# Layer 0's three later norms as small steps at fixed projection units, two engines' order written out over 17 units, and a bias load moved into attention

## The chip, the cores and the metric

The kernel runs on one core of a Trainium2 chip. The metric is the device time of one execution in microseconds, and the figure quoted is the median of the runs. Before the change it is 3485.43 us over three runs (3485.06 to 3486.84). The engines are called by the names of the profile: PE multiplies matrices, DVE does elementwise work and reductions, ACT evaluates functions and copies, POOL does small elementwise work, and SP and ACT also issue transfers.

## The reference

Two layers, each a pre-norm attention block and a pre-norm two-matrix block, over 2048 tokens of width 512. The same weights serve both layers:

```python
x = A_x                                    # (1, 2048, 512)
for _ in range(2):
    x = x + attention(layernorm(x), wqkv, wo)          # 32 heads of 16
    x = x + mish(layernorm(x) @ w1 + b1) @ w2          # inner width 1792
```

The layer norm subtracts the row's mean and divides by the root of its variance plus 1e-5. The bias `b1` is used only in the second block.

## The kernel before, in words

Every large product is made of three matmuls. An operand is split into a high part (a copy rounded to the matmul's type, on ACT) and a low part (the difference, on DVE), and high times high, high times low and low times high are summed (`mm3`, lines 159 to 164; `mm3_by_kind`, lines 152 to 157, does all four of the first kind, then all four of the second, then the third). `split_psum` (lines 148 to 150) makes both parts from a PSUM bank: one ACT copy, then one DVE subtraction.

The 2048 tokens are four chunks `c` of 512 (four row tiles of 128 each). Layer 0 begins with the projections. Each entry `(m, c)` of a list `order` is one unit: product `m` (0 to 3 are q, 4 to 7 are k, each 128 columns wide) of chunk `c`, 12 matmuls of 128x512 into one of three PSUM banks (tag "s"), a `split_psum` into a tile `pt`, and a transfer of `pt` to memory (`scr`). An entry `("v", c)` is four such blocks of 12 matmuls whose results go to `vst`. In layer 0 the list is: units 0 to 5 for chunk 0 (products 0, 4, 1, 5, 2, 6), units 6 to 9 for chunk 1 (0, 4, 1, 5), unit 10 (3, 0), units 11 and 12 for chunk 2 (0, 4), unit 13 (7, 0), units 14 and 15 for chunk 1 (2, 6), units 16 and 17 for chunk 3 (0, 4), then four more q and k units, the v blocks, and the rest.

A unit needs its chunk's normalised rows, transposed and split, as `th` and `tl`. So chunk 1's norm must be complete by unit 6, chunk 2's by unit 11, chunk 3's by unit 16. Chunk 0's norm is `first_norm` (from line 656, called at line 728), written out by hand. The norms of chunks 1 to 3 go through `norm_parts` (lines 166 to 202): first the statistics of all four row tiles (`bn_stats` and `bn_aggr`, lines 177 and 178), one small addition and one POOL power (lines 173 and 174), then for each row tile the subtraction and scaling `xn` (line 196), four PE transposes of 128x128 (line 201), and a `split_psum` into `th` and `tl`. `steps` hangs the parts on units: a part is written ahead of the unit with that number.

The raw weights are loaded by SP in pieces of 256 columns (`make`, line 115) into three buffers with the tag "raw", which the `pt` tiles share, and split on ACT (line 121) and DVE (line 126). The pieces 0 and 2 serve products 0, 1, 4 and 5; the pieces 1 and 3 serve products 2, 3, 6 and 7; the pieces 4 and 5 are v.

What each engine does next is decided by a planner when the program is built: it goes through a simulated time and gives each engine, among the instructions that it takes as ready, the one that stands first in the program. The chip then runs each engine's list in that order. An `Order` object ties each instruction passed to it behind the one passed before on the same engine, so that the planner cannot exchange them. `front` is such an object. Before the change it holds the first loads, all of `first_norm`, the split of the weight pieces 0 and 2, the matmuls of units 0 and 1, and the statistics (lines 177 and 178) of chunks 1 to 3. Everything else in the projections is left to the planner.

After 18 units the matmuls of the row maxima begin between the projections (`some_max`; lines 272, 290 and 305): they need `ks` and `qs`, which SP loads back from `scr`. Attention of layer 0 (`att.run`) follows: 512 steps, with an order written out for PE, DVE and ACT, and `hooks[s]` called at step `s`. The second block (`mlp`) then uses the bias tile `b1t` (line 598).

Of the kernel before, what the change touches and what calls it, by code (L numbers as in the profile page):

```python
# [18 lines left out]
P = 128  # L19
# [30 lines left out]
def kernel(ctx: ExitStack, tc: tile.TileContext, x, wqkv, wo, w1, b1, w2, out):  # L50
# [94 lines left out]
        nc.sync.dma_start(t.bitcast(F32), wparts[kind, j])  # L145
        return t

    def split_psum(hi, lo, src):
        nc.scalar.activation(hi, src, AF.Copy)
        nc.vector.tensor_tensor(lo, src, hi.bitcast(F32), op=ALU.subtract)  # L150

    def mm3_by_kind(acc, pairs, pe=lambda ins: ins):
        n = len(pairs)
# [12 lines left out]
    def norm_parts(src, nm, got, key, tag, fine=False, o=lambda ins: ins):  # L166
        st = tmp.tile([P, NCH, 6], F32, tag="st", name=f"st{nm}")
        mv = tmp.tile([P, NCH, 2], F32, tag="mv", name=f"mv{nm}")
        ve = tmp.tile([P, NCH], F32, tag="ve", name=f"ve{nm}")
        rs = tmp.tile([P, NCH], F32, tag="rs", name=f"rs{nm}")  # L170

        def rstd(t, n):
            nc.vector.tensor_scalar(ve[:, t : t + n], mv[:, t : t + n, 1], EPS, None, op0=ALU.add)
            nc.gpsimd.tensor_tensor(rs[:, t : t + n], ve[:, t : t + n], mhalf[:, t : t + n], op=ALU.pow)

        def stats(t):
            o(nc.vector.bn_stats(st[:, t], src[:, t]))
            o(nc.vector.bn_aggr(mv[:, t], st[:, t]))

        if not fine:  # L180
            for t in range(NCH):
                stats(t)
            rstd(0, NCH)
            yield
        th = b8([P, KT, CW], F32R, f"th{nm}")
        tl = b8([P, KT, CW], F32R, f"tl{nm}")
        got[key] = (th, tl)
        if fine:
            stats(0)
            rstd(0, 1)  # L190
        for t in range(NCH):
            if fine and t + 1 < NCH:
                stats(t + 1)
                rstd(t + 1, 1)
            xn = t512("f", f"xn{nm}{t}")
            nc.vector.tensor_scalar(
                xn, src[:, t], mv[:, t, 0:1], rs[:, t : t + 1], op0=ALU.subtract, op1=ALU.mult
            )
            tp = pbank(tag, f"tp{nm}{t}")
            for k in range(KT):  # L200
                nc.tensor.transpose(tp[:, ts(k, P)], xn[:, ts(k, P)], ident)
            split_psum(th[:, :, ts(t, P)], tl[:, :, ts(t, P)], tp.rearrange("p (k n) -> p k n", k=KT))
            yield
# [230 lines left out]
    def qkv(l, wts, tt, order, before, first=None, vst=None):  # L434
        scr = [dram.tile([2, P, S], F32R, name=f"scr{l}{m}") for m in range(2 * NCH)]
        vscr = dram.tile([NG, P, NKT, HG * VW], F32, name=f"vscr{l}")
        att = Attention(l, scr, vscr)
        if vst is None:
            vst = padded(l)
        chained = False  # L440
        done, left = 0, sum(NCH if m == "v" else 1 for m, _ in order)

        def some_max():
            nonlocal chained
            if done == 2 * NCH and left < AHEAD and att.nm < AHEAD:
                chained = True
                att.tick()
                att.max_pair()
                att.max_one()
                att.max_one()  # L450

        for i, (m, c) in enumerate(order):
            for fn in before.get(i, ()):
                fn()
            th, tl = tt[c]
            chained = chained or (l == 1 and i >= 11)
            pe = att.order if chained else lambda ins: ins
            if m == "v":
                for t in range(NCH):
                    acc = pbank("s", f"va{l}{c}{t}")  # L460
                    mm3(
                        acc,
                        [
                            (th[:, k, ts(t, P)], tl[:, k, ts(t, P)], wts[4 + k // 2][:, 0, k % 2], wts[4 + k // 2][:, 1, k % 2])
                            for k in range(KT)
                        ],
                        pe=pe,
                    )
                    left -= 1
                    st = vst[:, t % 2]  # L470
                    nc.scalar.activation(st[:, :, 0:DH], acc.rearrange("p (h d) -> p h d", d=DH), AF.Copy)
                    nc.sync.dma_start(
                        vscr[:, :, c * NCH + t, :].rearrange("g p n -> p g n"),
                        st.rearrange("p (g h) w -> p g (h w)", g=NG),
                    )
                    some_max()
            else:
                w = wts[m // 2]
                pt = tmp.tile([P, 2, CW], F32R, tag="raw", name=f"pt{l}{m}{c}", bufs=3)
                acc = pbank("s", f"qk{l}{c}{m}")  # L480
                (mm3_by_kind if l == 0 and i < 2 else mm3)(
                    acc,
                    [(w[:, 0, k, ts(m % 2, P)], w[:, 1, k, ts(m % 2, P)], th[:, k], tl[:, k]) for k in range(KT)],
                    pe=first if first and i < 2 else pe,
                )
                left -= 1
                split_psum(pt[:, 0], pt[:, 1], acc)
                nc.scalar.dma_start(
                    scr[m][:, :, ts(c, CW)].bitcast(F32).rearrange("a p n -> p a n"), pt.bitcast(F32)
                )  # L490
                if m in (0, 4):
                    done += 1
                    if done >= 2 * NCH - 2 and done % 2 == 0:
                        edge = (NCH - 1) * CW
                        for _ in att.prep_qk(0, *((edge, S) if done == 2 * NCH else (0, edge))):
                            pass
                some_max()
        att.prep_v(0)
        return att
# [152 lines left out]
    def steps(before, at, parts):  # L652
        for i in at:
            before.setdefault(i, []).append(lambda: next(parts, None))
# [69 lines left out]
    load_qkv(0, wts, (0, 2), later=splits, stores=stores, lo="dve", o=front)  # L724
    for c in range(1, NCH):
        xc.append(load_x(c, front))
    front(nc.sync.dma_start(b1t, b1.rearrange("(f p) -> p f", p=P)))
    first_norm(xc[0], tt, splits, front)
    wait = []
    load_qkv(0, wts, (1, 3), later=wait, stores=stores, lo="dve")  # L730
# [7 lines left out]
        at(i, lambda j=j: load_qkv(0, wts, (j,), later=wait, stores=stores, lo="dve"))  # L738
    for n in range(6):
        at(19 + n, lambda n=n: stores[n]())  # L740
    for c, at in ((1, range(1, 7)), (2, range(6, 12)), (3, range(11, 17))):
        steps(before, at, norm_parts(xc[c], f"q0{c}", tt, c, "n", o=front))
    for l in range(2):
        if l == 0:
            order = [(m, 0) for m in (0, 4, 1, 5, 2, 6)] + [(m, 1) for m in (0, 4, 1, 5)] + [(3, 0)]
# [25 lines left out]
        def divide(c):  # L771
            next(work[c], None)
# [18 lines left out]
        for c, load, inv, div in ((0, 30, 22, 20), (1, 28, 21, 15), (2, 10, 7, 5)):  # L791
            hooks[STEPS - load] = lambda c=c: behind(c, att.order)
            hooks[STEPS - inv] = lambda c=c: invert(c)
            for k in range(KT):
                hooks[STEPS - div + k] = lambda c=c: divide(c)
        att.run(hooks)
        o = att.order
        behind(3, o)
# [67 lines left out]
```

## Time and profile before

| | before |
|---|---|
| median of three runs | 3485.43 us |
| the profiled execution's own time | 3488.07 us |
| its span, first to last instruction | 3486.3 us |
| mean granted PE clock over the span | 0.997 |
| end of the first norm, start of the first projection matmul | 12.14 us |
| last projection matmul of layer 0, start of attention | about 178.3 us |

The page gives for each engine the busy time, then the span in 40 slices, the transfer queues, and the chain of work that ended last, followed back from the last instruction. A row of a timeline has the start, the duration, the engine, the line of the kernel, the operation, its output and inputs, their shapes, and a count (x4) where like instructions are merged; in square brackets stand the idle time of the engine before it and what ended it. PE's matmuls overlap, so the distance between two starts tells more than a duration. "PEclk" is the share of PE's full clock that was granted. "SPq" and "ACTq" rows are transfers being issued.

### The profile page before, as it was taken

What the parts mean: (1) busy time and instruction counts of PE and PEld (TensorE: products, weight loads), DVE (VectorE), ACT (ScalarE), POOL (GpSimd) and SP (SyncE); (2) the same over time, 40 slices, a digit from 0 to 9 for tenths busy, and PEclk for the clock granted to TensorE, in tenths of its full rate; (3) what the DMA queues carried; (4) which work ended last, traced back from release to release, by engine and by line L of the source; (5) the groups of instructions that cost most, each with busy time, mean ns of one, the idle gap of its engine ahead of it and who ended that gap; (6) DMA issues with size and microseconds to landing.
All of it is one profiled execution on the core that took longest, in us unless ns stands there. A gap on an engine that the chain in (4) does not pass through costs nothing.

```text
span 3486.3 us, 71314 instructions
## 1 busy us (share of the span) xinstructions
PE 3453.0 (99%) x29075; PEld 1916.8 (55%) x29075; DVE 3002.5 (86%) x4155; ACT 2554.8 (73%) x4781; POOL 444.2 (13%) x441
## 2 busy tenths in 40 slices
PE   9999999999999999999999999999999999999999
PEld 6644444444444444887776444444444444458887
DVE  5699999999999996666637999999999999966565
ACT  3189889889889987344421898988988998973444
POOL 1000000000000001344410000000000000013544
PEclk9999999999999999999999999999999999999999
DMA  7641312223122115400254202112020221154000
GB/s 248 230 97 44 81 42 74 51 63 80 45 57 51 34 55 133 168 13 13 85 191 162 52 15 46 25 36 38 23 55 15 45 35 27 55 149 152 13 13 25
DMA packets 131864, 247.40 MB, mean 71 GB/s; under 512 B 30928, under 2 KB 72400, under 8 KB 116432
## 3 DMA queue, kind: packets, MB, share of 16 engines
q1 hardware_dynamic: 110960, 186.21, 21.2%
q10 hardware_dynamic: 20576, 56.63, 4.2%
q8 instruction: 229, 3.75, 0.5%
q14 instruction: 99, 0.81, 0.1%
HBM read 149.43 MB, written 92.27 MB: 69 GB/s over the span
## 4 chain that ended last, share of the span: by engine, by line
DVE 71%; PE 19%; POOL 3%; DMA 2%; ACT 2%; issue 2%; SPq 0%; DVEq 0%; POOLq 0%; ACTq 0%
DVE mxv L305 32%; DVE mxv L290 32%; POOL hb L607 2%; DVE al L608 1%; PE qk L162 1%; PE h L163 1%; PE h L164 1%; PE mo L164 1%; PE h L162 1%; PE qk L163 1%; PE qk L164 1%; PE mo L162 1%; PE mo L163 1%; POOL hb L604 1%; PE va L162 1%
## 5 line engine op out<-in xcount | busy, mean ns | idle before, releaser
L354 ACT ACTIVATE p<-sp 128x512 f32<-128x512 f32 x4096 | 2134.9, 598 | 242.0 <-PE pn L272 138.9
L305 DVE TENSOR_REDUCE mxv<-pn 128x1 f32<-128x512 f32 x2048 | 1306.5, 677 | 13.0 <-PE pn L272 12.2
L290 DVE TENSOR_REDUCE mxv<-pm 128x2 f32<-128x1024 f32 x1024 | 1242.0, 1213 | 68.4 <-PE pm L272 68.2
L352 PE MATMUL sp<-qs,ks 50*128 50x512 f32 x4096 | 1293.2, 448 | 1.8 <-ACT p L354 1.6
L378 PE MATMUL pv<-p,va 128*32 128x256 f32 x16384 | 1200.1, 389 | 0.0
L352 PEld LDWEIGHTS sp<-qs,ks 50*128 50x128 f32 x4096 | 571.3, 184 | 714.5 <-ACT p L354 629.6
L272 PE MATMUL pn<-ks,qs 48*128 48x512 f32 x2048 | 826.0, 450 | 1.5 <-DVE mxv L305 1.5
L378 PEld LDWEIGHTS pv<-p,va 128*32 128x32 f32 x16384 | 378.4, 108 | 548.1 <-issue 432.6
L272 PE MATMUL pm<-ks,qs 48*128 48x512 f32 x2048 | 438.7, 423 | 2.0 <-DMA ks<-scr 1.2
L272 PEld LDWEIGHTS pn<-ks,qs 48*128 48x128 f32 x2048 | 365.7, 184 | 8.7 <-DVE mxv L305 3.0
L317 POOL CAST nh<-nm 128x16 fp32r<-128x16 f32 x64 | 12.7, 198 | 2394.4 <-DVE nm L312 2394.4
L272 PEld LDWEIGHTS pm<-ks,qs 48*128 48x128 f32 x2048 | 194.0, 185 | 66.5 <-issue 8.1
L162 PE MATMUL mo<-w,ah 128*128 128x512 f32 x448 | 176.9, 396 | 4.1 <-DVE ah L606 3.1
L604 POOL TENSOR_TENSOR hb<-hb,he 128x512 f32<-128x512 f32 x112 | 153.6, 1371 | 198.3 <-DVE he L601 195.0
L163 PE MATMUL mo<-w,ah 128*128 128x512 f32 x448 | 175.3, 391 | 0.0
L607 POOL TENSOR_TENSOR hb<-hb,hr 128x512 f32<-128x512 f32 x112 | 158.4, 1415 | 131.7 <-DVE ah L606 126.9
L163 PE MATMUL h<-tlm,w 128*128 128x512 f32 x448 | 174.7, 390 | 0.0
L164 PE MATMUL h<-thm,w 128*128 128x512 f32 x448 | 174.7, 390 | 0.0
L162 PE MATMUL h<-thm,w 128*128 128x512 f32 x448 | 174.6, 390 | 0.0
L600 ACT ACTIVATE he<-he 128x512 f32<-128x512 f32 x112 | 70.8, 632 | 137.3 <-DVE he L599 136.2
L602 ACT ACTIVATE hr<-he 128x512 f32<-128x512 f32 x112 | 70.9, 633 | 134.7 <-DVE he L601 74.5
L608 DVE TENSOR_TENSOR al<-hb,ah 128x512 fp32r<-128x512 f32 x112 | 103.8, 927 | 75.1 <-POOL hb L607 73.7
(130 smaller groups left out, 2601.2 us busy)
## 6 DMA issues: line engine op xcount, KB each, us to landing
scr<-pt ACTq DMA_DIRECT2D x64, 512.0 KB
ks<-scr SPq DMA_DIRECT2D x168, 128.0 KB
qs<-scr SPq DMA_DIRECT2D x168, 128.0 KB
vscr<-vst SPq DMA_DIRECT2D x32, 512.0 KB
va<-vscr SPq DMA_DIRECT2D x16, 1024.0 KB
w<-w1p SPq DMA_DIRECT2D x14, 1024.0 KB
w<-w2p SPq DMA_DIRECT2D x14, 1024.0 KB
raw<-ot SPq DMA_DIRECT2D x256, 32.0 KB
```

What stands on the lines that cost most here:

```text
L162: pe(nc.tensor.matmul(acc, ah, bh, start=first and i == 0, stop=False))
L163: pe(nc.tensor.matmul(acc, ah, bl, start=False, stop=False))
L164: pe(nc.tensor.matmul(acc, al, bh, start=False, stop=last and i == n - 1))
L272: nc.tensor.matmul(out, qs[h // 2][rows, q0 : q0 + P], ks[h // 2][rows, ts(c, 512)], start=True, stop=True)
L290: self.order(nc.vector.tensor_reduce(self.mxs[b][:, 0:2, qt, c], pm, axis=AX.X, op=ALU.max))
L305: self.order(nc.vector.tensor_reduce(self.mxs[b][:, h, qt, c : c + 1], pm, axis=AX.X, op=ALU.max))
L352: nc.tensor.matmul(sp, ks[h // 2][rows, ts(kt, P)], qs[h // 2][rows, ts(qb, CW)], start=True, stop=True)
L354: return lambda: self.order(nc.scalar.activation(self.pts[s][:, h], sp, AF.Exp, scale=SCALE))
L378: nc.tensor.matmul(acc[ts(h, VW), cols], va[:, kt, h, :], self.pts[s][:, h, cols], start=kt == 0 and half == 0, stop=kt == NKT - 1, skip_g ...
L604: nc.gpsimd.tensor_tensor(hb, hb, e, op=ALU.mult)
L607: nc.gpsimd.tensor_tensor(hb, hb, r, op=ALU.mult)
L608: nc.vector.tensor_tensor(al, hb, ah.bitcast(F32), op=ALU.subtract)
```

## The change

Five things are changed:

- The norms of chunks 1 to 3 use `norm_steps` (which the kernel already uses later on) in place of `norm_parts`. It works one row tile per step: four steps with `bn_stats`, `bn_aggr`, the small addition and the POOL power of one tile, then six steps in which step `t` makes `xn` of tile `t`, the low part of tile `t - 2`, and the transposes and high part of tile `t - 1`. All its DVE and PE instructions go through `front`.
- The steps stand at set units. Chunk 1's four statistics and its first `xn` are written ahead of unit 1, the other steps ahead of units 2 to 6.
- The matmuls of units 0 to 16 go through `front` (before: 0 and 1).
- The DVE low part of `pt` of units 0 to 16 goes through `front` (before: none).
- The load of `b1t` (line 727) leaves the head of the program, where it stood on SP behind the loads of x and ahead of the weight pieces 1 and 3, and is written at step 20 of layer 0's attention. There it is tied to nothing.

```diff
-    def split_psum(hi, lo, src):
+    def split_psum(hi, lo, src, o=lambda ins: ins):
         nc.scalar.activation(hi, src, AF.Copy)
-        nc.vector.tensor_tensor(lo, src, hi.bitcast(F32), op=ALU.subtract)
+        o(nc.vector.tensor_tensor(lo, src, hi.bitcast(F32), op=ALU.subtract))
...
-                    pe=first if first and i < 2 else pe,
+                    pe=first if first and i < 17 else pe,
...
-                split_psum(pt[:, 0], pt[:, 1], acc)
+                split_psum(pt[:, 0], pt[:, 1], acc, first if first and i < 17 else lambda ins: ins)
...
-    front(nc.sync.dma_start(b1t, b1.rearrange("(f p) -> p f", p=P)))
...
-    for c, at in ((1, range(1, 7)), (2, range(6, 12)), (3, range(11, 17))):
-        steps(before, at, norm_parts(xc[c], f"q0{c}", tt, c, "n", o=front))
+    for c, at in (
+        (1, (1, 1, 1, 1, 1, 2, 3, 4, 5, 6)),
+        (2, (4, 4, 5, 5, 6, 7, 8, 9, 10, 11)),
+        (3, (8, 8, 9, 9, 11, 12, 13, 14, 15, 16)),
+    ):
+        steps(before, at, norm_steps(xc[c], f"q0{c}", tt, c, "n", front))
...
+        if l == 0:
+            hooks[20] = lambda: nc.sync.dma_start(b1t, b1.rearrange("(f p) -> p f", p=P))
         att.run(hooks)
```

The function that now carries these norms, with the order in which it passes instructions to `o`:

```python
    def norm_steps(src, nm, got, key, tag, o):
        ...
        for t in range(NCH):
            o(nc.vector.bn_stats(st[:, t], src[:, t]))
            o(nc.vector.bn_aggr(mv[:, t], st[:, t]))
            o(nc.vector.tensor_scalar(ve[:, t : t + 1], mv[:, t : t + 1, 1], EPS, None, op0=ALU.add))
            nc.gpsimd.tensor_tensor(rs[:, t : t + 1], ve[:, t : t + 1], mhalf[:, t : t + 1], op=ALU.pow)
            yield
        ...
        for t in range(NCH + 2):
            if t < NCH:
                xns[t] = t512("f", f"xn{nm}{t}")
                o(
                    nc.vector.tensor_scalar(
                        xns[t], src[:, t], mv[:, t, 0:1], rs[:, t : t + 1], op0=ALU.subtract, op1=ALU.mult
                    )
                )
            if t >= 2:
                hi, sp = tps.pop(t - 2)
                o(nc.vector.tensor_tensor(tl[:, :, ts(t - 2, P)], sp, hi.bitcast(F32), op=ALU.subtract))
            if 1 <= t <= NCH:
                xn, tp = xns.pop(t - 1), pbank(tag, f"tp{nm}{t - 1}")
                for k in range(KT):
                    o(nc.tensor.transpose(tp[:, ts(k, P)], xn[:, ts(k, P)], ident))
                sp = tp.rearrange("p (k n) -> p k n", k=KT)
                hi = th[:, :, ts(t - 1, P)]
                nc.scalar.activation(hi, sp, AF.Copy)
                tps[t - 1] = (hi, sp)
            yield
```

## The prediction

> **What bounds the kernel now.** I read the page first, then the table by stage, then the waits of PE, then the chain of waits and the timeline of the first 40 us. The page:
>
> ```profile
> span 3486.3 us, 71314 instructions
> PE 3453.0 (99%) x29075; PEld 1916.8 (55%) x29075; DVE 3002.5 (86%) x4155; ACT 2554.8 (73%) x4781; POOL 444.2 (13%) x441
> DVE 71%; PE 19%; POOL 3%; DMA 2%; ACT 2%; issue 2%; SPq 0%; DVEq 0%; POOLq 0%; ACTq 0%
> ```
>
> The chain is DVE for 71% of the span, the row maxima of attention, which the change leaves alone. What it touches lies in the projections of layer 0. The table by stage, with busy time per engine and PE's granted clock:
>
> ```profile
> core 0: us, PE busy (x) PEld busy (x) DVE busy (x) ACT busy (x) POOL busy (x), PEclk, DMA share, GB/s
> 18.70:24.20 5.50, 5.50 (x25) 4.32 (x23) 3.87 (x8) 3.28 (x6) 1.02 (x1) 1.00 0.64 230
> 24.20:31.30 7.10, 6.79 (x34) 5.45 (x34) 7.10 (x15) 2.84 (x5) 0.00 (x0) 1.00 0.66 224
> 31.30:35.00 3.70, 1.78 (x12) 1.11 (x10) 3.47 (x10) 1.57 (x3) 1.01 (x1) 1.00 0.81 272
> 35.00:38.60 3.60, 3.60 (x9) 2.82 (x10) 2.97 (x8) 0.60 (x1) 0.45 (x1) 0.53 0.45 167
> 38.60:67.80 29.20, 29.20 (x145) 23.88 (x143) 14.77 (x24) 10.92 (x20) 0.55 (x1) 1.00 0.59 192
> 67.80:69.10 1.30, 0.09 (x2) 0.06 (x1) 0.69 (x1) 0.24 (x1) 0.00 (x0) 1.00 0.93 266
> 69.10:178.30 109.20, 109.20 (x478) 77.23 (x480) 65.50 (x86) 18.71 (x32) 0.42 (x2) 1.00 0.71 241
> 182.00:192.00 10.00, 9.73 (x55) 3.75 (x51) 7.43 (x10) 5.82 (x11) 0.00 (x0) 0.50 0.88 229
> ```
>
> The reader is to see that PE is the bound of this part: it is busy without a break from 69.1 to 178.3 us, so a microsecond that PE loses before 69 us reaches the end of the projections whole, and one saved does too. And there is little to save. PE idled 7.10 - 6.79 = 0.3 us near 24 us, 3.70 - 1.78 = 1.9 us near 33 us, ran 3.60 us at 0.53 of the clock (0.47 x 3.60 = 1.7 us lost), and idled 1.30 - 0.09 = 1.2 us near 68 us: 5.1 us in all, 0.15% of the span. About 0.2%, 7.0 us, is what a measurement of this kernel can tell from no change.
>
> PE's waits in that part name what ended them:
>
> ```profile
> PE pm L272 <- DMA ks<-scr: 1.2, 1, 1.2
> PE qk L162 <- ACT thq L149: 1.0, 1, 1.0
> PE qk L163 <- DVE tlq L150: 0.9, 1, 0.9
> ```
>
> The two in the middle of the loss are unit 6 waiting for the parts of chunk 1's norm. The wait of 1.2 us at 68 us is the first row maximum waiting for a transfer read back from memory; the change does not touch that, and I let it stand.
>
> **What the change removes.** If the norms arrive in time, 0.3 + 1.9 + 1.7 = 3.9 us go. The chain of waits shows why chunk 1 was late:
>
> ```profile
> 6.97 2.23 SPq L727
> 9.24 10.64 DMA qkr<-in_A_wqkv_dram
> 19.90 0.41 ACT qkm L121
> ```
>
> SP spent 2.23 us issuing the bias load, and the weight piece behind it, issued at 9.24, landed at 19.88. Without the bias load it can land up to 2.2 us earlier, at 17.7 to 19.9. DVE took it in this order:
>
> ```profile
> 3.59 0.69 DVE L675 BATCH_NORM_STATS2 stq<-x 128x6 f32<-128x512 f32 x1 [2.20 <-DMA x<-in_A_x_dram]
> 4.61 0.69 DVE L675 BATCH_NORM_STATS2 stq<-x 128x6 f32<-128x512 f32 x1
> 5.62 0.54 DVE L683 TENSOR_SCALAR xnq<-x,mvq,rsq 128x512 f32<-128x512 f32 x1
> 17.25 0.67 DVE L150 TENSOR_TENSOR pt<-qk,pt 128x512 fp32r<-128x512 f32 x1
> 21.09 1.23 DVE L126 TENSOR_TENSOR qkm<-qkr,qkm 128x1024 fp32r<-128x1024 f32 x1 [1.64 <-ACT qkm L121]
> 24.03 1.00 DVE L196 TENSOR_SCALAR xnq<-x,mvq,rsq 128x512 f32<-128x512 f32 x2
> 29.56 1.22 DVE L126 TENSOR_TENSOR vm<-vr,vm 128x1024 fp32r<-128x1024 f32 x1
> ```
>
> DVE stood 1.64 us at the weight piece with `xn` of chunk 1 behind it, so `xn` came at 24.03.
>
> **What the change adds, first: a gap ahead of unit 2.** This is the step that decides. Unit 0's low part of `pt` is now in the same DVE order as the norm, and it is written ahead of chunk 1's statistics; the first transposes of chunk 1 are now in PE's order, ahead of unit 2. So unit 2 waits for: unit 0, its `pt`, four statistics steps, `xn`, the transposes. PE and ACT in the trace of before:
>
> ```profile
> 6.21 0.66 PE L689 MATMUL tpq<-ident,xnq 128*128 128x128 f32 x4 [1.01 <-DVE xnq L683]
> 14.06 1.19 PE L157 MATMUL qk<-tlq,qkm 128*128 128x512 f32 x4 [0.72 <-DVE tlq L695]
> 16.19 0.60 ACT L149 ACTIVATE pt<-qk 128x512 fp32r<-128x512 f32 x1 [3.06 <-PE qk L157]
> 17.80 0.39 PE L162 MATMUL qk<-thq,qkm 128*128 128x512 f32 x1
> 18.03 0.39 PE L163 MATMUL qk<-tlq,qkm 128*128 128x512 f32 x1
> 33.27 0.73 PE L162 MATMUL qk<-thq,qkm 128*128 128x512 f32 x2 [0.98 <-ACT thq L149]
> ```
>
> PE's side: from 14.06, 20 of the 24 matmuls of units 0 and 1 remain, 0.23 us apart (17.80 to 18.03), so PE is through with them at 14.06 + 20 x 0.23 = 18.7. DVE's side: ACT ends the high part at 16.79, the low part takes 0.67, to 17.5; four steps as in the first norm, 4.61 - 3.59 = 1.02 each, to 21.5; from the start of `xn` to the transposes 6.21 - 5.62 = 0.59, to 22.1. A gap of 3.4 us. Before, DVE did these statistics while unit 0 was still on PE, and PE ran units 2 and 3 meanwhile (5.50 of 5.50 us busy from 18.7 to 24.2). That cover is gone: the order forbids unit 2, and of the work left free only v blocks need nothing but chunk 0, and their first weight piece was split at 29.56 + 1.22 = 30.8.
>
> The weight piece's low part, 1.23 us, is tied to nothing and stands in the program ahead of the statistics. If it falls among them, the gap is 4.7 us. If the planner puts it ahead of unit 0's `pt`, DVE waits for the landing, at worst 18.9, with two ACT halves inside; then 18.9 + 1.23 + 0.67 + 4.08 + 0.59 = 25.5, a gap of 6.8 us. I take 4.7: in the trace this low part did run ahead of chunk 1's `xn`, and with the piece landing earlier it need not stand still.
>
> **Second, the clock.** In the stage from 31.3 to 35.0 us PE idled 1.9 of 3.7 us, and the next 3.6 us had 0.53 of the clock, 1.7 us lost. A gap of 4.7 us is longer than that, so I add 1.7 us; the bounds are 0 and 3.4 (one such stage more). [...]
>
> **Third, three hand-overs.** The last low part of a chunk's norm is now behind the `pt` of the unit just before the unit that needs it (units 6, 11, 16). From that unit's last matmul: ACT 0.60, `pt` 0.67, the low part another 0.67, less one matmul of 0.23 that needs high parts alone: 1.7 us each. What can fill them is the v blocks, free and ready from 30.8 us on for half a block, 6 x 0.23 = 1.4 us, which leaves 0.3; I take 0.3 for each, 1.0 for the three. Bounds: 0, and 3 x 1.7 = 5.1 if nothing fills them.
>
> **Fourth, the same work in other pieces.** DVE gets nine more small additions and POOL nine more powers. Those of chunk 1 are in the 1.02 us steps counted above; those of chunks 2 and 3 fall where DVE was busy 14.77 of 29.20 us (38.6 to 67.8), which hides them; bare they would be a part of 1.02 us each.
>
> **Fifth, the bias load's new place.** Its rows:
>
> ```profile
> 183.95 0.37 SPq L115 DMA_DIRECT2D w1r<-in_B_w_dram  x1
> 208.79 1.69 SPq L329 DMA_DIRECT2D rows<-nt  x4
> 230.89 1.38 SPq L248 DMA_DIRECT2D ks<-scr  x3
> 246.36 1.69 SPq L329 DMA_DIRECT2D rows<-nt  x4
> L598 ACT ACTIVATE hb<-h,b1t x112: 670/689/692, 1421.1 to 3472.0; 128x512 f32<-128x512 f32 x112
> ```
>
> A block of 16 steps takes 246.36 - 208.79 = 37.6 us, so step 20 is near 178.3 + 47 = 225 us. SP is free from 232.3 to 246.4 us, where 2.23 us fit ahead of the next rows; the first reader comes at 1421.1. Nothing. If it stands in front of other loads there, those wait 2.2 us, with blocks of 37.6 us to spare.
>
> **The sum.** 4.7 + 1.7 + 1.0 - 3.9 = 3.5 us slower. The profiled execution took 3488.07 us, 2.6 more than the median of the runs, 3485.43; I carry the difference over to the median: 3488.9 us.
>
> **The rivals.**
>
> (a) *The stalls go and nothing takes their place.* Then 3.9 us go, and 1.2 more if the row maxima start later than their transfer: 3480.3 us. For it speaks that DVE no longer stands 1.64 us at the weight piece; against it, that the order alone forces 3.4 us. It is faster by over 0.2% only if the half-clock stage from 182 to 192 us also vanishes, where DVE was idle 10.00 - 7.43 = 2.6 us: 3477.7 us.
>
> (b) *The written order becomes the bound: the hand-overs at units 6, 11 and 16 are not filled, and each is followed by a half-clock stage as at 35 us.* 4.7 + 1.7 + 3 x (1.7 + 1.7) - 3.9 = 12.7 us slower, 3498.1 us. It decides from 4.5 us in the hand-overs on, two bare ones and one half-clock stage: that is where the sum passes 7.0 us. For it: at unit 6 before, planned by the same planner, PE issued two matmuls and then idled (33.27, x2), with nothing else put in. Against it: the v piece had been split only at 30.8 us, and later there is more free work. [...]
>
> (c) *The bias load is not moved into attention.* Tied to nothing, it can be given to SP as soon as SP is free. For it speaks the row at 183.95: that load is written at step 78, near 178.3 + 78 x 37.6 / 16 = 362 us, and it went out 178 us earlier. If it goes right behind the weight piece 1, that piece still gains its 2.2 us and piece 3 does not: the sum holds within 1 us, so this rival shares the forecast's time, 3488.9 us.
>
> **How the numbers follow.** The forecast with its small variants has 0.67, and of that (c) is true in about two cases of three. Rival (a) has 0.10, of which 0.03 reach faster by over 0.2%. Rival (b) has 0.17. The other 0.06 is a plan that comes out differently later on with no net effect. Faster 0.03, same 0.67 + 0.07 + 0.06 = 0.80, slower 0.17. The low end is the bare gap with no clock lost, the wait at 68 us gone and the half-clock stage at 182 us too: 3.4 - 3.9 - 1.2 - 2.6 = -4.3, 3481. The high end is the longest gap, one half-clock stage and all hand-overs bare: 6.8 + 1.7 + 5.1 - 3.9 = 9.7, 3495. Outside lie the rest of (a), about 0.07, and the upper half of (b), about 0.09.
>
> **What the profile after would show.** Right: PE idle for 3.4 to 4.7 us from about 18.7 us, ended by DVE `xn` and followed by a stage at half clock; no wait for `th` and `tl` at unit 6 of over 1 us; v matmuls between the q and k units from about 35 us; the projections ending near 182 us, and the same distance from there to the end. Wrong: transposes of chunk 1 before 20 us (no gap), or PE idling 1.7 us in front of units 6, 11 and 16 each (rival b), or a difference that arises behind 200 us.

## The result, and the profile after

The kernel after takes 3518.91 us (median of five runs, 3517.37 to 3521.19), the kernel before 3485.39 us on the same chip (3483.40 to 3486.84). The ratio is 1.0095, 95% interval 1.0084 to 1.0105: 33 us slower. The forecast was 3488.9 us and its range ended at 3495. The profiled execution after took 3520.42 us. Its page, first the span, then busy time per engine, then the shares of the chain that ended last:

```profile
span 3518.6 us, 71334 instructions
PE 3463.3 (98%) x29075; PEld 1924.4 (55%) x29075; DVE 3003.7 (85%) x4164; ACT 2554.3 (73%) x4781; POOL 448.4 (13%) x450
DVE 1%; PE 1%; POOL 1%; ACT 0%; issue 0%; POOLq 0%; DVEq 0%; ACTq 0%
```

The span is 32.3 us longer, the busy times hardly so: time in which nothing ran was added. The chain is followed back for only some 3% of the span here, so it can't say where the time went. The start of attention can. The first exponential of attention, in the timeline of before and of after:

```profile
178.92 1.78 ACT L354 ACTIVATE p<-sp 128x512 f32<-128x512 f32 x3 [0.29 <-PE sp L352]
```

```profile
210.74 1.78 ACT L354 ACTIVATE p<-sp 128x512 f32<-128x512 f32 x3 [0.29 <-PE sp L352]
```

31.8 of the 32.3 us are there already: all of it is lost in layer 0's projections. The table by stage of after (same columns as in the prediction):

```profile
core 0: us, PE busy (x) PEld busy (x) DVE busy (x) ACT busy (x) POOL busy (x), PEclk, DMA share, GB/s
18.70:24.20 5.50, 1.62 (x8) 1.00 (x6) 5.36 (x13) 2.81 (x5) 1.22 (x3) 1.00 0.49 182
24.20:31.30 7.10, 5.69 (x16) 4.67 (x17) 2.24 (x6) 0.60 (x1) 1.21 (x2) 0.54 0.48 148
...
44.10:50.00 5.90, 5.87 (x21) 4.72 (x22) 1.46 (x3) 1.61 (x3) 0.00 (x0) 0.71 0.24 92
...
63.40:75.00 11.60, 9.18 (x43) 7.21 (x43) 2.64 (x5) 2.77 (x5) 0.00 (x0) 1.00 0.51 171
75.00:92.00 17.00, 8.91 (x28) 6.65 (x29) 4.47 (x7) 1.69 (x3) 0.00 (x0) 0.60 0.70 149
...
130.50:138.00 7.50, 5.90 (x16) 4.11 (x16) 0.00 (x0) 1.79 (x3) 0.00 (x0) 0.54 1.01 345
138.00:178.30 40.30, 40.30 (x180) 27.57 (x179) 27.15 (x34) 7.19 (x12) 0.00 (x0) 1.00 0.60 187
```

Before, PE was busy without a break from 69.1 to 178.3 us. Now there are holes near 20, 80 and 131 us, and the stages from 24.20, 75.00 and 130.50 us, behind or around them, have 0.54, 0.60 and 0.54 of the clock. PE's waits from 12 to 215 us name them (us in total, times, longest):

```profile
PE pm L272 <- DMA ks<-scr: 8.5, 2, 7.6
PE tpq L578 <- DVE xnq L568: 5.3, 1, 5.3
PE va L162 <- ACT vst L471: 4.9, 1, 4.9
PE qk L163 <- DVE tlq L574: 4.3, 2, 2.5
PE tpq L578 <- DVE tlq L574: 2.0, 1, 2.0
PE pn L272 <- DVE mxv L305: 1.3, 3, 0.8
PE sp L352 <- ACT p L354: 0.7, 1, 0.7
PE qk L157 <- DVE tlq L695: 0.7, 1, 0.7
PE qk L157 <- ACT thq L691: 0.3, 1, 0.3
```

These rows add up to 28.0 us; the same list of before adds up to 6.1, so 21.9 us more are waits (22.4 when each list ends at its first exponential, 26.8 against 4.4). Lost clock is estimated from the table as PE's busy time times the missing share: 0.46 x 5.69 + 0.29 x 5.87 + 0.40 x 8.91 + 0.46 x 5.90 = 10.6 us, against 1.7 us before (at 35 us), so 8.9 us more. The first projection matmul starts 1.5 us later. 21.9 + 8.9 + 1.5 = 32.3 us, against 31.8 us seen at the first exponential: the loss is accounted for within about 1 us. The second row is the gap that was forecast, the fourth the hand-overs. The first, third and fifth, 15.4 us, are in no case of the prediction.

**The head of SP's queue.** The timeline of after: the bias load is the first transfer of the program, ahead of x, and the first projection matmul starts at 13.60 us (before: 12.14 us).

```profile
0.74 0.45 SPq L800 DMA_DIRECT2D b1t<-in_B_b_dram  x1
...
13.60 1.20 PE L157 MATMUL qk<-thq,qkm 128*128 128x512 f32 x4 [0.26 <-ACT thq L691]
```

**The gap ahead of unit 2.** DVE does two low parts of weight pieces (L126) among chunk 1's four statistics, then `xn`, and PE waits for it, all in the timeline of after:

```profile
20.71 1.23 DVE L126 TENSOR_TENSOR qkm<-qkr,qkm 128x1024 fp32r<-128x1024 f32 x1
...
22.51 1.21 DVE L126 TENSOR_TENSOR qkm<-qkr,qkm 128x1024 fp32r<-128x1024 f32 x1
...
24.92 0.54 DVE L568 TENSOR_SCALAR xnq<-x,mvq,rsq 128x512 f32<-128x512 f32 x1
...
25.61 1.09 PE L578 MATMUL tpq<-ident,xnq 128*128 128x128 f32 x4 [5.29 <-DVE xnq L568]
```

**The hole near 80 us.** It has to do with the loads that read `ks` and `qs` back. In before the first goes out at 59.64 us, and the first row maximum waits 1.21 us (timeline of before):

```profile
59.64 2.41 SPq L248 DMA_DIRECT2D qs<-scr  x5
...
69.07 0.46 PE L272 MATMUL pm<-ks,qs 48*128 48x512 f32 x1 [1.21 <-DMA ks<-scr]
```

In after the loads start 11 us later, since the chunk 2 units whose result they read are later. That alone need not cost more. From the first load to the first maximum it takes 9.4 us in before (59.64 to 69.07 us) and 9.3 us in after (70.89 to 80.16 us). What differs is the work between: in before, units 14 and 15 and the last two groups of chunk 3's transposes stand behind unit 13 and ahead of the first half of the maximum in PE's list; in after, both halves stand directly behind unit 13, ahead of the third group of chunk 3's transposes. Why the planner put them there is not shown. From the timeline of after, by engine (SP, PE, DVE, ACT):

```profile
70.89 2.97 SPq L248 DMA_DIRECT2D qs<-scr  x6
...
80.16 0.76 PE L272 MATMUL pm<-ks,qs 48*128 48x512 f32 x1 [7.58 <-DMA ks<-scr]
...
82.68 1.23 DVE L290 TENSOR_REDUCE mxv<-pm 128x2 f32<-128x1024 f32 x1 [11.49 <-PE pm L272]
83.82 0.68 DVE L574 TENSOR_TENSOR tlq<-tpq,thq 128x512 fp32r<-128x512 f32 x1
84.42 0.68 DVE L150 TENSOR_TENSOR pt<-qk,pt 128x512 fp32r<-128x512 f32 x1
...
85.13 0.41 ACTq L488 DMA_DIRECT2D scr<-pt  x1
85.77 0.60 ACT L581 ACTIVATE thq<-tpq 128x512 fp32r<-128x512 f32 x1 [12.55 <-PE tpq L578]
```

PE stands 7.58 us at the row maximum; DVE stands 11.49 us at its reduction, with a low part `tl` and a `pt` behind it; ACT stands 12.55 us ahead of a store and a `th`. Here both wait for what stands behind the maximum: the store goes out at 85.13 us, when DVE has ended its `pt` at 85.10, and the `th` follows its transposes, issued at 84.64 us.

**The hole near 131 us.** SP's second batch of these loads stands in its queue for a long time, the v stores come behind it, the tile `vst` has two slots, and PE waits for a bank that ACT can't empty (timeline of after; the first v store of before went out at 98.39 us):

```profile
84.43 22.76 SPq L248 DMA_DIRECT2D qs<-scr  x7
...
128.41 11.64 SPq L472 DMA_DIRECT2D vscr<-vst  x6
...
131.45 0.60 ACT L471 ACTIVATE vst<-va 128x512 f32<-128x512 f32 x1 [8.12 <-DMA vscr<-vst]
...
132.10 0.80 PE L162 MATMUL va<-vm,thq 128*128 128x512 f32 x1 [4.95 <-ACT vst L471]
```

### The profile page after: what moved, and what is told of

It is laid out like the page before. It is cut to its first block, busy times and chain, and to the rows that moved or that the text cites. A ratio compares the mean times of both kernels' runs of the same rounds, so it can differ in the third digit from the quotient of the medians.

```text
span 3518.6 us, 71334 instructions
## 1 busy us (share of the span) xinstructions
PE 3463.3 (98%) x29075; PEld 1924.4 (55%) x29075; DVE 3003.7 (85%) x4164; ACT 2554.3 (73%) x4781; POOL 448.4 (13%) x450
```

## The experiments

The theory after the result: there are two groups of losses. The gap and the hand-overs, at 20 to 65 us, cost what they take. They also make chunk 2's units late, so the read-back loads are late, and what stands behind these loads stops next: the maxima in PE's list, the stores on ACT, the v stores on SP. Rivals: one cause makes all the rest (the bias load, the gap, or the maxima); or the ties, or the small steps, cost by themselves. Each run gives a median and, from its profile, the time of the first exponential of attention, which is free of what happens later. Such a time comes from one execution: the first projection matmul starts between 12.85 us (pool_both) and 13.60 us (after) in kernels with the bias load at the head, so a difference of about 1 us between two of these times is not told apart. Before is measured with every group of runs (medians 3484.67 to 3486.39 us); medians of different groups can differ by that much without a cause.

| run | median us | ratio to before, 95% interval | first exponential us |
|---|---|---|---|
| before | 3485.39 | | 178.92 |
| after | 3518.91 | 1.0095 (1.0084 to 1.0105) | 210.74 |
| b1_alone | 3489.29 | 1.0010 (1.0001 to 1.0019) | 181.62 |
| b1_held | 3490.28 | 1.0012 (1.0002 to 1.0021) | 181.82 |
| after_b1_held | 3519.76 | 1.0095 (1.008 to 1.011) | 209.18 |
| after_max_held | 3512.69 | 1.0075 (1.006 to 1.009) | 205.71 |
| after_units_free | 3507.15 | 1.0059 (1.0042 to 1.0075) | 199.52 |
| after_parts | 3501.58 | 1.0045 (1.003 to 1.006) | 193.01 |
| after_gap_later | 3517.28 | 1.0090 (1.0073 to 1.0107) | 205.44 |
| after_loads_pool | 3505.53 | 1.0053 (1.0038 to 1.0068) | 190.69 |
| max_stores_pool | 3503.47 | 1.0047 (1.003 to 1.0064) | 193.45 |
| after_vstores_pool | 3515.76 | 1.0079 (1.0064 to 1.0094) | 203.98 |
| free_loads_pool | 3498.84 | 1.0033 (1.0021 to 1.0044) | 185.60 |
| before_loads_pool | 3488.39 | 1.0004 (0.9994 to 1.0013) | 178.50 |
| pool_gap_later | 3500.85 | 1.0045 (1.003 to 1.006) | 189.24 |
| pool_low_early | 3496.59 | 1.0032 (1.002 to 1.0043) | 183.71 |
| pool_both | 3495.44 | 1.0028 (1.0017 to 1.0039) | 182.38 |

### The bias load: b1_alone, after_b1_held, b1_held

The kernel before with only the bias load moved (b1_alone):

```diff
-    front(nc.sync.dma_start(b1t, b1.rearrange("(f p) -> p f", p=P)))
...
+            hooks[20] = lambda: nc.sync.dma_start(b1t, b1.rearrange("(f p) -> p f", p=P))
```

> The kernel before, with the bias load alone moved as in the change. Theory: the load floats to the head of SP as in the changed kernel, the start is 1.5 us later, and nothing else is lost: 3485 to 3487. Rival (the early bias load is a large part of the 33 us): over 3492.

And the load kept at its place in attention, in after (after_b1_held) and in before (b1_held):

```diff
-            hooks[20] = lambda: nc.sync.dma_start(b1t, b1.rearrange("(f p) -> p f", p=P))
+            hooks[20] = lambda: tc.keep_in_program_order(nc.sync.dma_start(b1t, b1.rearrange("(f p) -> p f", p=P)))
```

> The changed kernel, with the bias load tied behind what is written ahead of it on SP, so that it stays in attention. Theory (the written order costs most, the bias load at the head of SP a little): the first projection matmul comes at 12.1 us again instead of 13.6, so 1.5 us less than the changed kernel, 3517.4, and all later waits stay. Rival (the early bias load disturbs the loads behind it and so causes the late norms): 5 us less or more, 3513 or below.

> The kernel before with the bias load written at step 20 of attention and kept in program order there, so that it can't float to the head of SP's queue. Theory (the load at the head of SP costs 1.45 us of start, and its place ahead of weight piece 1 costs up to 2.2 us): unit 0 starts at 12.1 us, weight piece 1 lands up to 2.2 us earlier, DVE's stop of 1.64 us goes; 0 to 3 us less than before, 3482 to 3486 us. Rival (the projections run by what the planner makes of it, and any shift of a few us gives another order): within 5 us of before on either side, with other waits than before's near 25, 33 and 68 us.

Moved alone, the load costs 2.7 us at the first exponential and 2.9 us in the median (3486.39 us for before in the same group): more than the 1.5 us expected, and far less than the rival's. Held in place, the first projection matmul of after is back at 12.12 us, and the first exponential comes 1.6 us earlier, but the wait for `xn` grows from 5.3 to 6.9 us: `xn` comes at 25.09 instead of 24.92 us, because the weight piece that DVE must split ahead of it lands at about the same time, 19.7 us. Nothing is gained in the median, and neither of the two times expected came. In before it doesn't help either (+2.9 us at the first exponential, and 3490.28 us where 3482 to 3486 were expected): the planner then orders the transposes and low parts of chunk 1 otherwise, and PE waits 2.2 us for them, as the rival had it. The bias load is a cause of about 3 us, not of 32.

### The row maxima: after_max_held

The maxima are tied behind unit 16 on PE and DVE, so that they leave the list of the 17 units:

```diff
+            if first and i == 17:
+                att.order.last.update({e: v for e, v in first.last.items() if e in (nc.tensor.engine, nc.vector.engine)})
```

> The changed kernel, with the row maxima tied behind unit 16 on PE and DVE, so that they cannot be put into the written order. Theory (a maximum put between units 13 and 15 waits for a transfer that comes late, and holds the norm of chunk 3 behind it): the waits of 7.6, 0.9, 1.3 and 2.0 us go, and with them most of the half-clock stage from 76 to 90 us, about 4 us: 14 us less than the changed kernel, 3505; 3500 if the wait of 4.9 us for the v stores goes too. Rival (the transfers themselves are late, and whoever comes first waits): at most 3 us less, the same wait at a later matmul.

6.2 us less, 5.0 at the first exponential: between the 14 us of the theory and the 3 us of the rival. The waits for `ks` are gone, but the next in line wait. PE's waits of this kernel (its code is two lines longer, so later line numbers are two higher), and from its timeline the `pt` of unit 13 on DVE, then ACT:

```profile
PE qk L162 <- ACT thq L583: 4.5, 1, 4.5
...
PE qk L162 <- DVE pt L150: 4.0, 1, 4.0
```

```profile
74.17 0.69 DVE L150 TENSOR_TENSOR pt<-qk,pt 128x512 fp32r<-128x512 f32 x1 [1.48 <-ACT pt L149]
...
82.39 0.37 ACTq L490 DMA_DIRECT2D scr<-pt  x1
82.81 0.60 ACT L583 ACTIVATE thq<-tpq 128x512 fp32r<-128x512 f32 x1 [8.66 <-DMA ks<-scr]
...
87.67 0.37 ACTq L490 DMA_DIRECT2D scr<-pt  x1
88.14 0.60 ACT L149 ACTIVATE pt<-qk 128x512 fp32r<-128x512 f32 x1 [3.76 <-DMA scr<-pt]
```

Here no row maximum holds anything, and still ACT stood 8.66 us. The trace has the landing of a `ks` load as its end, a load which neither the `th` nor the store ahead of it reads, and the `pt` of unit 13 had been complete since 74.17 + 0.69 = 74.86 us. The store of unit 13 goes out at 82.39 us, and the `th` that PE needs stands behind it on ACT. The store of unit 14 goes out at 87.67 us, and the 3.76 us that ACT idled there end with the landing of a store of `pt`. What makes a store on ACT wait for a load on SP no trace shows; that the store is what held ACT is the next run's question.

### The stores on ACT: max_stores_pool

The same kernel, with the stores of `pt` issued by POOL. PE's list is the same matmul for matmul in all of layer 0:

```diff
-                nc.scalar.dma_start(
+                nc.gpsimd.dma_start(
                     scr[m][:, :, ts(c, CW)].bitcast(F32).rearrange("a p n -> p a n"), pt.bitcast(F32)
```

> The kernel with the maxima held behind unit 16 (3512.69 us; first exponential of attention at 205.7 us), with one thing changed: the stores of pt to scr go out from POOL in place of ACT. PE's order is the same matmul for matmul. [...] First exponential 10 to 13 us earlier, at 193 to 196 us; 3499 to 3503 us. Rival (th and pt are late because their own transposes and matmuls are, and ACT only waits for them): waits and time unchanged within 3 us, 3510 to 3516 us.

9.2 us less than after_max_held and 12.3 us at the first exponential, inside the 10 to 13 expected there (the median is 0.5 us above its range). The wait for `vst`, 3.0 us in after_max_held, falls to 1.2. ACT's timeline of this kernel:

```profile
73.71 0.60 ACT L149 ACTIVATE pt<-qk 128x512 fp32r<-128x512 f32 x1 [2.13 <-PE qk L164]
74.20 0.59 ACT L583 ACTIVATE thq<-tpq 128x512 fp32r<-128x512 f32 x1
```

The `th` that follows unit 13's `pt` comes at 74.20 in place of 82.81 us, and of the waits of 4.5 and 4.0 us only 1.0 us for `pt` is left. This is the largest step in this order of removal: stores on ACT behind loads of SP. In after itself the maximum held the same store (85.10 us, above), so the two losses lie in the same stretch of time, and how much of the 17.3 us is due to which was not separated.

### The v stores: after_vstores_pool

```diff
-                    nc.sync.dma_start(
+                    nc.gpsimd.dma_start(
                         vscr[:, :, c * NCH + t, :].rearrange("g p n -> p g n"),
```

> The kernel after with one thing changed: the stores of the v blocks (vst to vscr) go out from POOL in place of SP, so that they don't stand behind the read-back loads in SP's queue. PE's order is the same. Theory: PE's wait of 4.9 us for vst near 131 us goes, and the half-clock stage of 6.8 us behind it; everything ahead of 100 us stays. First exponential 5 to 8 us earlier, at 203 to 206 us; 3511 to 3514 us. Rival (the v blocks are held by the store's own time or by the same loads in the transfer engines, not by the queue): within 2 us of after.

PE's wait for `vst`, 4.9 us in after, is gone, the first exponential is 6.8 us earlier, inside what was expected; the median is only 3.2 us lower, 1.8 us short of it. That the wait came with the v stores' place on SP is shown, the size in the median is at the edge of what the runs tell apart.

### The loads themselves: after_loads_pool, before_loads_pool, free_loads_pool

The other side of the same pair: the stores stay, and the read-back loads of the first group go to POOL. `prep_qk` takes the issuing engine as an argument here (its own lines are left out).

```diff
-                    for _ in att.prep_qk(0, *((edge, S) if done == 2 * NCH else (0, edge))):
+                    for _ in att.prep_qk(0, *((edge, S) if done == 2 * NCH else (0, edge)), eng=nc.gpsimd):
```

> The kernel after, with one thing changed: the loads that read ks and qs back for the first group of heads go out from POOL's queue in place of SP's. [...] The maxima are then also out of the written order, as the program puts them behind unit 17. Forecast 15 to 22 us less than after, 3497 to 3504 us. Rival (the maxima in the written order are the whole loss there, and the queue of the loads is nothing): as with the maxima held behind unit 16, 3512 us, and PE still waits 3 to 4.5 us each for th, pt and vst. Third possibility: POOL issues 48 transfers so slowly that the first maxima come much later, which shows as maxima missing beside the v blocks and a longer attention; then 3515 us or more.

13.4 us less in the median, a little short of the 15 to 22 expected, and 20.0 us at the first exponential. What is left of PE's waits above 1 us in this kernel:

```profile
PE tpq L579 <- DVE xnq L569: 5.3, 1, 5.3
PE qk L163 <- DVE tlq L575: 4.3, 2, 2.5
PE pn L273 <- DVE mxv L306: 1.3, 3, 0.5
PE qk L162 <- DVE pt L150: 1.0, 1, 1.0
```

All three unforeseen waits are gone, the forecast ones stay. The planner also put the maxima behind unit 17 here, without a tie, so this run alone does not tell the queue from the place of the maxima; after_max_held and max_stores_pool do.

> The kernel before with the loads of ks and qs from POOL: the control for the other runs with these loads on POOL. Theory (in before the loads come early enough that little stands behind them: one wait of 1.2 us): first exponential within 2 us of before's 178.9 us, 3483 to 3488 us. Rival (POOL's queue is better in itself, whatever the order, or moves the maxima away from the front, which is worth something in itself): 10 us or more less than before.

The control: in before the same move changes nothing at the first exponential (178.50 against 178.92 us). So POOL's queue is not better in itself: in the order of before the loads on SP cost nothing there, in that of after they cost 20 us.

> The kernel after with units 2 to 16 untied (3507.15 us, first exponential at 199.5 us), and besides the loads of ks and qs from POOL. Theory (all that is lost behind 60 us, in either order, is the work that stands behind these loads): PE's waits of 7.3 us (pm for ks), 4.4 us (va for vst), 3.2 us and 2.0 us (th, pt) and the half-clock stages at 75 and 120 us go; first exponential at 181 to 185 us, level with before with the bias load moved (181.6 us); 3487 to 3492 us. Rival (the norms in small steps at late units cost by themselves): first exponential at 188 us or later, with waits for th and tl at units 6, 11 and 16.

With units 2 to 16 untied as well, the first exponential comes at 185.60 us, just outside the 181 to 185 expected, with waits of 2.9 us for `th` and 2.6 us for `pt`; the median is 7 us above the expected end. Most of what the small steps cost without ties was again behind the loads (199.52 to 185.60 us), but not all.

### Ties or steps: after_units_free, after_parts

Units 2 to 16 untied, in after (steps alone), and, in the other run, the old norms with the ties kept (ties alone):

```diff
-                    pe=first if first and i < 17 else pe,
+                    pe=first if first and i < 2 else pe,
...
-                split_psum(pt[:, 0], pt[:, 1], acc, first if first and i < 17 else lambda ins: ins)
+                split_psum(pt[:, 0], pt[:, 1], acc)
```

```diff
-        steps(before, at, norm_steps(xc[c], f"q0{c}", tt, c, "n", front))
+        steps(before, at, norm_parts(xc[c], f"q0{c}", tt, c, "n", o=front))
```

with the unit numbers of before in the second. 

> The changed kernel, with the matmuls of units 2 to 16 and all low parts of pt left to the planner again; the norms keep their new steps and order. Theory: the gap of 5.3 us ahead of unit 2 and its half-clock stage go, and the hand-overs at units 6 and 11 too, 12 us less at least: 3507 or below. Rival (the small steps themselves, with their statistics and powers one by one, make the norms late): as the changed kernel within 4 us.

> The kernel after with the norms of chunks 1 to 3 as before (statistics of all four tiles first, parts at units 1 to 6, 6 to 11, 11 to 16), but with the matmuls and low parts of units 0 to 16 still tied and the bias load moved: the ties alone. With the kernel that has the steps alone (3507, no ties) and before with the bias load moved (3489, neither), this fills the table of four. Theory (two causes that feed the same losses: steps at late units make chunks 2 and 3 late, ties forbid PE other work meanwhile): no gap ahead of unit 2, the transposes of a chunk all directly ahead of the unit that needs them, so waits of 2 to 4 us at units 6 and 11, and the maxima stand behind unit 17 without blocking a norm; 3493 to 3503 us. Rival (the ties are the cause, whatever the norm's pieces): 3510 to 3519 us. Other rival (the steps alone are the cause): 3487 to 3491 us.

Against b1_alone (181.62 us at the first exponential), the steps alone cost 17.9 us, the ties alone 11.4, both 29.1. Neither half is the cause by itself; the medians are at or within what the theory had (3507 us or below for the steps, 3493 to 3503 us for the ties). Of the 17.9 us of the steps alone 13.9 lie behind the loads, as free_loads_pool shows; for the ties alone the loads were not moved. With the ties alone the maxima are behind unit 17, and PE waits 5.9 us for `vst` and 4.2 us at chunk 1's transposes.

### The gap and the hand-overs: after_gap_later, pool_gap_later, pool_low_early, pool_both

Chunk 1's first transposes one unit later, in after and in after_loads_pool:

```diff
-        (1, (1, 1, 1, 1, 1, 2, 3, 4, 5, 6)),
+        (1, (1, 1, 1, 1, 1, 3, 3, 4, 5, 6)),
```

> The kernel after with chunk 1's first transposes written ahead of unit 3 in place of unit 2 (and the second ones there too), all else the same: unit 2 can cover 2.8 us of the gap of 5.3 us. Theory (each stop costs for itself, and the later ones come from the order of the maxima, the stores and the loads): the gap falls to about 2.5 us and its half-clock stage from 6.8 to 3.4 us, 4.5 us less; the stops near 76 and 131 us stay; 3513 to 3516 us. Rival (the gap makes everything behind it late and so causes the later stops): the stops near 76 and 131 us shrink too, 3500 us or less.

> The kernel after with the loads of ks and qs from POOL (3505.53 us, first exponential of attention at 190.7 us), and chunk 1's first transposes written ahead of unit 3 in place of unit 2. Theory (what is left behind the loads is the sum of the gap ahead of unit 2, the hand-overs and their half-clock stages, each for itself): the gap of 5.3 us falls to 2.5 us and its stage from 6.8 to 3.4 us; first exponential 4.5 to 6 us earlier, near 185.5 us; 3499 to 3501 us. Rival (a stop saved early only makes the next one longer): hand-overs of over 4.3 us in all, first exponential at 188 us or later.

In after the first exponential is 5.3 us earlier and the stops near 76 and 131 us stay, as the theory has it, though the median falls by 1.6 us only, to 1.3 us above its range. From the timeline of after_gap_later, SP and PE:

```profile
65.14 2.90 SPq L248 DMA_DIRECT2D qs<-scr  x6
...
74.49 0.76 PE L272 MATMUL pm<-ks,qs 48*128 48x512 f32 x1 [7.05 <-DMA ks<-scr]
```

The loads start 5.75 us earlier than in after, and the maximum still waits 7.05 us: how late the loads come is not what sets this wait. Without the loads in the way (pool_gap_later) it gains only 1.5 us at the first exponential, less than the 4.5 to 6 expected: PE waits 2.8 and 1.1 us for the first two `xn` in place of 5.3 once. The gap was split, not covered.

The last low part of each chunk one unit earlier (with the loads on POOL), then both edits:

```diff
-        (1, (1, 1, 1, 1, 1, 2, 3, 4, 5, 6)),
-        (2, (4, 4, 5, 5, 6, 7, 8, 9, 10, 11)),
-        (3, (8, 8, 9, 9, 11, 12, 13, 14, 15, 16)),
+        (1, (1, 1, 1, 1, 1, 2, 3, 4, 5, 5)),
+        (2, (4, 4, 5, 5, 6, 7, 8, 9, 10, 10)),
+        (3, (8, 8, 9, 9, 11, 12, 13, 14, 15, 15)),
```

> The kernel after with the loads of ks and qs from POOL, and the last low part of the norms of chunks 1, 2 and 3 written one unit earlier (ahead of units 5, 10, 15 in place of 6, 11, 16), so that it stands ahead of the low part of pt of the unit before the one that needs it. Theory (the hand-overs are the place of this low part behind pt): PE's waits of 2.5 and 1.8 us for tl at units 6 and 11 fall below 1 us each and the half-clock stage of 3.4 us at 44.7 us goes; the gap ahead of unit 2 stays at 5.3 us with its stage; first exponential 3 to 6 us earlier, at 185 to 188 us; 3499 to 3503 us. Rival (the transposes themselves come too late, so the waits only change their name from tl to th): within 1.5 us of 190.7 us.

> Both edits together, with the loads from POOL. Theory (the terms add): first exponential near 181 us, level with before with the bias load moved (181.6 us); 3488 to 3494 us: the whole of the change's loss is then gone with the 17 units still tied and the norms still in small steps. Rival (ties or small steps cost something of their own beside these places): 185 us or later.

pool_low_early gains 7.0 us at the first exponential and 8.9 us in the median (7.8 us when each is taken against before in its own group), more than expected. Its only wait over 1.3 us among the units is that of the gap:

```profile
PE tpq L579 <- DVE xnq L569: 5.6, 2, 5.3
```

The hand-overs were the place of one low part behind `pt`: 4.3 us of waits, 1.0 for `pt` behind them, and about 1.6 us of lost clock (estimated as above, from 0.93 of the clock over 22.17 us of busy PE between 44 and 68 us in after_loads_pool) make 6.9 of the 7.0. In pool_both the first exponential is at 182.38 us, 0.8 us from b1_alone, with all ties and all small steps in place and 4.7 us of waits left at the gap: in sum they cost nothing there that these times can tell. Its median is 1.4 us above the range expected and still 10.8 us above before; 3.5 us of that are at the first exponential, 2.3 us is what before_loads_pool, with the same loads on POOL, loses at the end of the program (below), and the rest lies in between, within the spread of its runs (3488.57 to 3498.66 us). No run is faster than before.

## Why the prediction was wrong

**The step that failed** is the sentence "The wait of 1.2 us at 68 us is the first row maximum waiting for a transfer read back from memory; the change does not touch that, and I let it stand." The change does touch it. The loads take as long as before, 9.3 us from the first issue to the first maximum, but the new lists put the maximum, the stores on ACT and the v stores behind them with too little work between: the maximum alone waits 7.58 us in place of 1.21, and with the loads on POOL 20.0 us are gone. At the first exponential:

| step | us | run against run |
|---|---|---|
| bias load moved | 2.7 | b1_alone, before |
| ties, steps and the smaller gap, rest | 0.8 | pool_both, b1_alone |
| gap, as far as one unit can cover it | 1.3 | pool_low_early, pool_both |
| hand-overs | 7.0 | after_loads_pool, pool_low_early |
| v stores and what else is behind the loads | 2.8 | max_stores_pool, after_loads_pool |
| stores on ACT behind the loads | 12.3 | after_max_held, max_stores_pool |
| maxima in the written order | 5.0 | after, after_max_held |

Before rounding they add up to 31.8 us, as they must, since each row is the difference of two neighbours in one sequence of kernels; 20.0 of it is behind the loads. The v stores by themselves are worth 6.8 us when taken out of after, so the three lower rows overlap: their sum is one measured difference, their shares hold for this order of removal. The rows of 0.8 and 1.3 us are near what the starts differ by (13.59 us in b1_alone, 13.43 in pool_low_early, 12.85 in pool_both). No rival had the loads as a cause, though a 1.2 us wait for them stood in the quoted rows. A wait of that size did not say that the load was cheap: 8 of its 9.4 us were hidden behind other work.

**The gap ahead of unit 2** was right in its mechanism: 4.7 us forecast with one weight low among the statistics, 5.3 us measured with two of them there. **The clock** behind it was forecast at 1.7 us and cost 0.46 x 5.69 = 2.6 by the estimate above (0.54 granted from 24.2 to 31.3 us).

**The hand-overs** were mis-sized: 1.0 us forecast, 7.0 measured. "What can fill them is the v blocks" failed. In both kernels' lists PE has no v matmul ahead of unit 17; the first starts at 86.9 us before and at 112.5 us after. Why the planner put nothing there is not shown. Rival (b) had this place, at 3.4 us for each of three bare hand-overs with a half-clock stage, 10.2 us; two were bare, and only that at unit 6 had the stage. The bare price of 1.7 us fits unit 11; at unit 6, ACT's copy of unit 5 waited some 0.4 us for a free tile (41.78 us), and a statistic of chunk 2 (41.77 us) held DVE's `pt` for another 0.4. At unit 6 (2.53 us of idle) the stage from 44.1 to 50.0 us has 0.71 of the clock; at unit 11 (1.78 us) the next stage has 1.00. The third hand-over, at unit 16, shows no wait for `tl` in after: behind unit 16's first matmul PE had row maxima and a later unit (93.9 to 96 us), not v blocks.

**The bias load** went as rival (c) said, but to the head of SP's queue, ahead of x, and not behind weight piece 1. The first projection matmul came 1.5 us later for it, where the prediction gave it no cost of its own. That it was then worth nothing to hold it back was not foreseen: the weight piece, not x, sets `xn` of chunk 1. The 2.2 us that this piece was to gain didn't come (19.88 us before, about 19.5 after), so the 18.9 us that the prediction took as the worst case for its longest gap was not the worst.

**The removed stalls**, 3.9 us, went in name only: DVE's stop of 1.64 us at the weight piece is gone, but the gap took the place of the wait near 24 us, and one wait of 2.53 us that of the 1.0 and 0.9 us at unit 6.

**The signs** named for "wrong" did show: PE idling in front of units 6 and 11. The sign "the same distance from there to the end" also held: 31.8 us at the first exponential, 32.3 at the end of the span.

## What to carry to other kernels

When an order is written out, list for every engine what stands next in its queue, its stores too, and ask what each of these waits for if the work ahead comes some microseconds later; ACT issued a store here and also made the next operand, and PE's waits of 4.5 and 4.0 us behind ACT's 8.66 us in after_max_held fell to 1.0 us with the stores on POOL. A short wait for a load in the trace of before says only how much work stood between its issue and its use (here 8 of 9.4 us); in a new order, count that work again. Ties take away the planner's other work, so each hand-over inside them must be hidden by the order itself (here by one low part, one unit earlier).

## What the runs showed of the hardware that was not expected

A store on ACT went out only after loads on SP that it does not read: ACT idled 8.66 us in after_max_held until a `ks` load had landed, and this idle time is not there with the stores on POOL (in max_stores_pool the `th` behind unit 13's `pt` comes at 74.20 in place of 82.81 us). What ties the two transfers is not shown. The 12.55 us that ACT idled in after are not such a case: DVE, behind the row maximum, ended the `pt` of that store only at 85.10 us.

With the read-back loads on POOL, before_loads_pool ends later after its last matmul than before does. The last matmul of before and of before_loads_pool in their timelines:

```profile
3481.33 0.40 PE L164 MATMUL mo<-w,al 128*128 128x512 f32 x1
```

```profile
3480.48 0.40 PE L164 MATMUL mo<-w,al 128*128 128x512 f32 x1
```

The spans end at 3486.3 and 3487.8 us: 5.0 and 7.3 us after the start of that matmul, 2.3 us more with 48 loads of each layer on POOL. What of the loads makes the difference was not tried.
